# A Fourier filter followed by a maxout layer: new PSUM tiles and order for the opening, and another way out for the last output tile

## The chip, the cores and the metric

The kernel runs on one core of one Trainium2 chip. The metric is device time in microseconds of one execution; lower is better. The time before is the median of four runs.

## The reference

For each of 8 sequences (3072 positions, 256 channels) the reference filters along the sequence in the frequency domain, and the result then goes through a layer of two projections whose elementwise maximum is projected back.

```python
X = np.fft.rfft(x, axis=1)                      # x: 8 x 3072 x 256
F = (filt_r + 1j * filt_i)[None, :, :]          # 1537 x 256
y = np.fft.irfft(X * F, n=x.shape[1], axis=1)
y = y.reshape(8 * 3072, 256)
h1 = y @ w1                                     # 256 x 1024
h2 = y @ w2
out = np.maximum(h1, h2) @ w_out                # 1024 x 256
```

## The kernel before

**The mathematics.** A sequence of length 3072 is taken as 128 x 24. The transform is a product with a 128 x 128 table of sines, a second stage with 48-row tables (`U`), the filter as a product on the vector engine, and two stages back (tables `VP`, `VQ`, then `G1`, the transpose of `C1`). The maximum is computed as relu(y (w1 - w2)) w_out + y (w2 w_out). So the kernel needs `Wd` = w1 - w2 and `M` = w2 w_out, which it makes itself at the start, as it makes all tables.

**The engines.** TensorE (PE) does all products and transposes into PSUM. ScalarE (ACT) and VectorE (DVE) copy results out of PSUM. GpSimd (POOL) makes index patterns, does a few products and conversions at the start, and issues the loads of `x` and the weights and all writes of the output. SyncE (SP) issues the writes and reads of the intermediate arrays `ad`, `bt`, `zd`, `zr`. Each engine works through its own queue in the order in which the code calls it (the schedule is written by hand), and waits there for what the other engines have not finished.

**The opening (sequence 0).** While tables and data arrive, the first sequence is transformed without a trip through DRAM:

- `table_c` makes `C1` on ACT by four sine instructions, and DVE then copies it in another order to `Ct`. `tables_u` makes the angles of the second table on DVE, `sines_u` its sines on ACT.
- `expand_f(g, ri, E)` spreads 2 x 2 rows of the filter over the partitions: 16 matmuls into a PSUM tile `pf`, which engine E copies to `F`. `ri` is 0 for the real and 1 for the imaginary part.
- `first_s1(c)` is the first stage for tile c of `x` (8 matmuls into `pa`), copied to `At` by ACT. `first_t1(g, E)` transposes one group of it (8 transposes into `pt`), copied to `bt` by E.
- `tables_pe` and `tables_q` make `VP` and `VQ` (PSUM tiles `pv` and `pw`).
- `first_s2(g, pool)` is the second stage of one of 8 groups (8 matmuls into `px`). `px` holds two products, k = 0 and 1, each 2 KB per partition. They are multiplied with `F` by DVE; for three of the groups the k = 1 product is copied out by ACT to `xs` and multiplied by POOL.
- `first_s3(g, pq)` is the way back into `pz`, copied to `Zt` by ACT, behind a filler matmul (`spin`). `first_t2(j, E)` transposes `Zt` to `zr`.
- `prep_w(k, E)` transposes w2 (k = 0, 1) and multiplies it with w_out (k = 2, 3) to give `M`. `table_g` makes `G1`. On POOL, `fix_f` repairs some rows of `F`, and `prep_wd` makes w2 in bf16 and `Wd`.

**PSUM in the opening.** [...] `bank2` hands out tiles of 4 KB in two tags, `pa` and `pb`, two buffers each. Before the loop over groups the two tags take turns, so that four tiles rotate; in the loop `px` uses `pb` and everything else uses `pa`. A tile can be written again when the last reader of its predecessor has finished.

```python
ring = ["pa", "pb"]
def bank2(shape, dtype, name, tag=None):
    if tag is None:
        ring.append(ring.pop(0))
        tag = ring[-1]
    return p2.tile(shape, dtype, tag=tag, name=name)
```

**The steady part.** It has 48 output tiles of 512 rows (`tt`), 8 steps each (`j`). In each step `moe_h` computes one eighth of the hidden layer (`ph`, then `gt`) and `moe_o` a part of the previous tile's output (`po`, then `ot`). Between them, at steps that are written into `todo`, lie the transforms of later sequences: `f1` (first stage, twelve pieces, each two of which are written to `ad` by SP), `f1_read` (four reads into `bt`), `gen_f2` (second stage, filter and way back), `z_read`, and `s4`, the last stage of the transform for one tile. `f1(1, c)` is the first stage of sequence 1: four of its pieces stand before step 0, eight in steps 0 to 4, its `f1_read` at step 5, and its second stage from step 18.

**The end.** `moe_o` copies half a tile to `ot` at j = 3 and the other half at j = 7. After the second, POOL writes the 512 KB tile to the output. Behind the last tile the program ends with drains and barriers of all engines (line 733).

Of the kernel before, what the change touches and what calls it, by code (L numbers as in the profile page):

```python
# [8 lines left out]
FP32 = mybir.dt.float32  # L9
BF16 = mybir.dt.bfloat16  # L10
# [3 lines left out]
B = 8  # L14
N = 3072
D = 256
# [13 lines left out]
def kernel(  # L30
# [52 lines left out]
    init = setup.enter_context(tc.tile_pool(name="init", bufs=1))  # L83
    p2 = setup.enter_context(tc.tile_pool(name="p2", bufs=2, space=bass.MemoryType.PSUM))
    ctx.enter_context(tc.manual_schedule())
    ring = ["pa", "pb"]

    def bank2(shape, dtype, name, tag=None):
        if tag is None:
# [3 lines that stand above are left out]
# [20 lines left out]
    def expand_f(g, ri, E):  # L113
        pf = bank2([128, 2, 2, D], FP32, "pf")
        for b in range(2):
            for i in range(2):
                u = 2 * g + i
                for c in range(2):
                    for dr in range(2):
                        m, o = 4 * b + c, u  # L120
                        if dr:
                            m, o = (7 - m, 16 - u) if u else (7 - m + c, 0)
                        p0 = 64 * c + 32 * dr
                        TE.matmul(pf[p0:p0 + 32, b, i], Sel[:, m], Fs[ri][:, o], start=True, stop=True)  # L124
        evac(E, F[:, ri, :, 2 * g:2 * g + 2].rearrange("p b u d -> p b (u d)"), pf.rearrange("p b u d -> p b (u d)"))
# [62 lines left out]
    def table_c():  # L188
        V.memset(kc[:, :, 1, 0:1], 32.0)
        V.memset(kc[:, 1, 0, 0:1], 64.0)  # L190
        p128 = init.tile([128, 1], FP32)
        V.tensor_scalar(p128, pid, 1.0 / 128.0, None, OP.mult)
        uc = init.tile([128, 2, 2, T], FP32)
        rc = init.tile([128, 2, 2, T], FP32)
        V.tensor_scalar(uc[:, 0], kc[:, 0], p128, 0.25, OP.mult, OP.add)
        V.tensor_scalar(uc[:, 1], kc[:, 1], p128, 0.5, OP.mult, OP.add)
        V.tensor_scalar(uc[:, 1, 0, 0:1], kc[:, 1, 0, 0:1], p128, 0.25, OP.mult, OP.add)
        V.tensor_scalar(rc, uc, RND, RND, OP.add, OP.subtract)
        V.tensor_tensor(uc, uc, rc, OP.subtract)
        Cv = C1.rearrange("p (h c u b a) -> p a b c h u", h=4, c=2, b=2, a=2)  # L200
        for a in range(2):
            for b in range(2):
                S.activation(Cv[:, a, b], uc[:, a, b].rearrange("p (c h u) -> p c h u", c=2, h=4),
                             AF.Sin, bias=zero, scale=TWO_PI)

        V.tensor_copy(Ct.rearrange("p (b a t) -> p t b a", b=2, a=2), C1.rearrange("p (t b a) -> p t b a", b=2, a=2))

    def tables_u():

# [82 lines left out]
    def table_g():  # L292
        pg = bank2([128, 128], BF16, "pg")
        TE.transpose(pg, C1, I128)
        S.activation(G1, pg, AF.Copy)
# [132 lines left out]
    def zeros(out_, n):  # L428
        S.activation(out_, zero.rearrange("p (a b) -> p a b", a=1).to_broadcast([128] + n), AF.Copy)

    def first_s1(c):
        pa = bank2([128, 2, 2, 2, 4, T], FP32, "pa")
        for dh in range(2):
            for n in range(4):
                TE.matmul(pa[:, dh, :, :, n], xb[0, c][:, n, 128 * dh:128 * dh + 128],  # L435
                          Ct.rearrange("p (b a t) -> p b a t", b=2, a=2), start=True, stop=True)
        S.activation(At[:, :, 0:48].rearrange("p h (a n) t -> p h a (n t)", a=2)[:, :, :, 128 * c:128 * c + 128],
                     pa.rearrange("p h b a n t -> p (h b) a (n t)"), AF.Copy)

    def first_t1(g, E):  # L440
        pt = bank2([128, 2, 2, D], BF16, "pt")
        t0 = 8 * (g // 2) + 2 * (g % 2)
        for c in range(2):
            for i in range(2):
                for dh in range(2):
                    TE.transpose(pt[:, c, i, 128 * dh:128 * dh + 128],
                                 At[:, 2 * dh:2 * dh + 2].rearrange("p b m t -> p t (b m)")[:, t0 + 4 * c + i], I128)
        o = bt[0][0:ROWS, 8 * (g // 2):8 * (g // 2) + 8].rearrange("p (c u) d -> p c u d", c=2)[:, :, 2 * (g % 2):2 * (g % 2) + 2]
        evac(E, o.rearrange("p c u d -> p c (u d)"), pt[0:ROWS].rearrange("p c u d -> p c (u d)"))

    def evac(E, out_, in_):
        if E is V:
            V.tensor_copy(out_, in_)  # L453
        else:
            S.activation(out_, in_, AF.Copy)  # L455

    def first_s2(g, pool):
        px = bank2([128, 2, 2, D], FP32, "px", "pb")
        for i in range(2):
            for k, c in QUADS:  # L460
                t_ = 8 * (g // 2) + 4 * c + 2 * (g % 2) + i
                TE.matmul(px[64 * c:64 * c + 64, k, i], U[64 * k:64 * k + 48, t_],
                          bt[0][64 * k:64 * k + 48, t_], start=True, stop=True)
        if pool:
            xs = apool.tile([128, 2, D], FP32, tag="at", name="xs")
            S.activation(xs[0:FROWS], px[0:FROWS, 1], AF.Copy)  # L466
        pq = []
        for k in range(2):
            pq.append(pqpool.tile([128, 2, 2, D], BF16, tag="pq", name="pq"))
            E, src = (G, xs) if k and pool else (V, px[:, k])  # L470
            E.tensor_tensor(pq[k][0:FROWS],  # L471
                            src[0:FROWS].rearrange("p (o i) d -> p o i d", o=1).to_broadcast([FROWS, 2, 2, D]),
                            F[0:FROWS, :, k, 2 * g:2 * g + 2], OP.mult)
        return g, pq
# [58 lines left out]
    def moe_o(tt, j):  # L533
        n, half = divmod(j, 2)
        y_, g_ = yt[tt], gt[tt]
        if j == 0:
            ot[tt] = opool.tile([128, 4, D], FP32, tag="ot", name="ot")
        if j % 4 == 0:
            po[tt] = pso.tile([128, 2, D], FP32, tag="po", name="po")
        p_ = po[tt][:, n % 2]  # L540
        if half == 0:
            for dc in range(2):
                TE.matmul(p_, y_[:, dc, n], M[:, dc], start=(dc == 0), stop=False)  # L543
            js = range(0, 3)
        else:
            js = range(3, 8)
        for jj in js:
            TE.matmul(p_, g_[:, jj, 128 * n:128 * n + 128], Wo[:, jj], start=False, stop=(jj == 7))  # L548
        if j % 4 == 3:
            V.tensor_copy(ot[tt][:, n - 1:n + 1], po[tt])  # L550
        if j == 7:
            b, i = divmod(tt, 6)
            dst = out[b * N:(b + 1) * N].rearrange("(p n) d -> p n d", n=N2)
            G.dma_start(out=dst[:, 4 * i:4 * i + 4], in_=ot[tt])  # L554


    def drain(g):
# [18 lines left out]
    order = (1, 2, 3, 0, 4, 5, 6, 7)  # L576
    expand_f(1, 0, S)
    expand_f(2, 0, S)
    first_s1(0)
    expand_f(3, 0, V)  # L580
    first_s1(1)
    sines_u(0)
    expand_f(0, 0, V)
    first_s1(2)
    sines_u(1)
    expand_f(4, 0, V)
    first_s1(3)
    sines_u(2)
    expand_f(5, 0, V)
    first_s1(4)  # L590
    tables_pe()
    first_s1(5)
    tables_q(0, S)
    first_t1(1, V)
    first_t1(2, V)
    tables_q(1, S)
    first_t1(3, V)
    expand_f(1, 1, S)
    first_t1(0, V)
    expand_f(2, 1, S)  # L600
    pend = []
    ring = ["pa"]
    for n, g in enumerate(order):
        if n < 4:
            first_t1(order[n + 4], V)
        pend.append(first_s2(g, n in (0, 2, 4)))
        if n in (1, 3):
            expand_f(6 + n // 2, 0, S)
        if n < 6:
            expand_f(order[n + 2], 1, S)  # L610
        if n == 0:
            load_wo()
        if n == 1:
            fix_f()
        if n in (1, 3, 5):
            prep_wd(n // 2, *wf)
        if n > 1:
            first_s3(*pend.pop(0))
        if n in (4, 5):
            prep_w(n - 4, S)  # L620
        if n == 4:
            table_g()
        if n == 6:
            prep_w(2, S)
            prep_w(3, S)
    first_s3(*pend.pop(0))
    first_s3(*pend.pop(0))
    zr[0] = zrpool.tile([128, N2, D], BF16, tag="zr", name="zr")
    f1(1, 0, V)
    f1(1, 1, V)  # L630
    first_t2(0, V)
    setup.close()
    ps = ctx.enter_context(tc.tile_pool(name="ps", bufs=6, space=bass.MemoryType.PSUM))
    pso = ctx.enter_context(tc.tile_pool(name="pso", bufs=2, space=bass.MemoryType.PSUM))
    ypool = ctx.enter_context(tc.tile_pool(name="ypool", bufs=3))
    gpool = ctx.enter_context(tc.tile_pool(name="gpool", bufs=2))
    opool = ctx.enter_context(tc.tile_pool(name="opool", bufs=2))
    f1(1, 2, S)
    s4(0)
    f1(1, 3, V)  # L640

    todo = {}

    def plan(step, fn, *a):
        todo.setdefault(step, []).append((fn, a))
# [25 lines left out]

    for j in range(1, 6):
        plan(j - 1, first_t2, j, V)
    for c in range(4, 12):
        plan(int(0.6 * (c - 3)), f1, 1, c, (S, V)[c % 2])
    plan(5, f1_read, 1)
    plan_f2(1, spaced(18, 1.8, 9), 28, 34)
    plan_x(2, spaced(8, 4, 6))
    plan_f1(2, spaced(34, 1, 12), 46)
# [58 lines left out]
```

## Time and profile before

| | |
|---|---|
| Median of four runs | 542.48 us (541.70 to 543.44) |
| Profiled execution, its own time | 543.44 us |
| Its span in the profile | 541.5 us |
| PE busy | 512.2 us (95%) |
| ACT busy | 337.6 us (62%) |
| DVE busy | 322.3 us (60%) |
| POOL busy | 72.5 us (13%) |
| First ph matmul (step 0) | 54.44 us |
| Last output DMA issued by POOL | 531.85 us |

The span is the time from the first to the last record of the core; 1.95 us of the execution's own time lie outside it. A busy share is an average over stages: the opening, up to about 54 us, and the end behind the last matmul have to be read by themselves. Matmul ends are modelled in the profile.

### The profile page before, as it was taken

To read this page: it belongs to the slowest core of one execution; us is meant where nothing else is said; L and a number is where in the kernel's file an instruction comes from. 1 tells how busy PE (TensorE), PEld (TensorE's weight loads), DVE (VectorE), ACT (ScalarE), POOL (GpSimd) and SP (SyncE) were. 2 spreads that over 40 slices of the span, in tenths; PEclk is the share of its full clock that TensorE was granted. 3 is DMA by queue.
4 is the path that set the end of the run, shared out by engine and by line. 5 is a ranking of instruction groups with operands and counts; after the bars stand their busy time and mean duration, and the time that the engine had idled before them with its cause. 6 is when DMAs were issued, how large, how long until landed. Compare 5 with 4: busy or idle time off the path is not lost.

```text
span 541.5 us, 12518 instructions
## 1 busy us (share of the span) xinstructions
PE 512.2 (95%) x5359; PEld 349.6 (65%) x5359; DVE 322.3 (60%) x427; ACT 337.6 (62%) x591; POOL 72.5 (13%) x126
## 2 busy tenths in 40 slices
PE   6887999999999999999999899999999999999992
PEld 3655666666667666676667566666667666677771
DVE  8676669435863576448764677338764687344331
ACT  6786747865786578745775467745775565555540
POOL 6193011011101200021001200021000000000000
PEclk9799999999999999999999999999999999999997
DMA  8973496879478956599468947599466935611111
GB/s 158 286 123 61 130 164 144 206 243 207 115 231 220 216 144 186 154 220 205 122 212 207 209 117 203 149 212 209 121 204 180 170 91 134 166 40 79 79 40 77
DMA packets 67596, 87.07 MB, mean 161 GB/s; under 512 B 3986, under 2 KB 48276, under 8 KB 66452
## 3 DMA queue, kind: packets, MB, share of 16 engines
q1 hardware_dynamic: 51908, 44.31, 36.5%
q0 software_dynamic: 15632, 41.95, 29.3%
q8 instruction: 42, 0.69, 0.5%
q14 instruction: 14, 0.11, 0.1%
HBM read 53.74 MB, written 47.19 MB: 186 GB/s over the span
## 4 chain that ended last, share of the span: by engine, by line
issue 66%; POOL 6%; PE 4%; POOLq 0%
POOL out_dram L554 4%; POOL xb L101 2%; PE po L548 1%; PE ph L523 1%; PE po L543 0%; PE px L411 0%; PE py L507 0%; POOLq L733 0%; POOLq L554 0%; PE pz L392 0%; POOLq L101 0%
## 5 line engine op out<-in xcount | busy, mean ns | idle before, releaser
L528 ACT ACTIVATE gt<-ph 128x512 bf16<-128x512 f32 x307 | 181.8, 599 | 110.9 <-PE ph L523 110.0
L548 PE MATMUL po<-Wo,gt 128*128 128x256 bf16 x1536 | 229.8, 273 | 0.0
L548 PEld LDWEIGHTS <-gt 128*128 128x128 bf16 x1536 | 150.3, 98 | 57.5
L416 DVE TENSOR_TENSOR pq<-px,F 120x1024 bf16<-120x1024 f32 x112 | 131.6, 1217 | 25.6 <-PE px L411 24.7
L550 DVE COPY ot<-po 128x512 f32<-128x512 f32 x96 | 66.2, 690 | 109.4 <-PE po L548 108.8
L396 ACT ACTIVATE zt<-pz 112x512 bf16<-112x512 f32 x112 | 60.7, 594 | 45.8 <-PE pz L392 40.7
L523 PEld LDWEIGHTS <-Wd 128*128 128x128 bf16 x768 | 69.9, 98 | 25.3 <-issue 11.1
L554 POOL DMA_DIRECT2D out_dram<-ot x48 | 25.8, 537 | 442.9 <-DVE ot L550 415.6
L526 DVE TENSOR_SCALAR gt<-ph 128x512 bf16<-128x512 f32 x77 | 52.8, 686 | 35.6 <-PE ph L523 31.6
L455 ACT ACTIVATE at<-pa 128x512 bf16<-128x512 f32 x77 | 46.2, 600 | 10.5 <-PE pa L357 9.0
L357 PE MATMUL pa<-xb,C 128*128 128x512 bf16 x84 | 31.5, 381 | 1.4 <-DVE zr L453 0.8
L507 PE MATMUL py<-G,zr 128*128 128x128 bf16 x384 | 29.7, 219 | 0.7 <-DVE pq L416 0.7
L392 PE MATMUL pz<-pq,VP 56*64 56x256 bf16 x448 | 28.8, 272 | 1.6 <-DVE pq L416 1.6
L507 PEld LDWEIGHTS <-zr 128*128 128x128 bf16 x384 | 24.9, 98 | 6.0 <-issue 3.5
L392 PE MATMUL pz<-pq,VQ 56*64 56x256 bf16 x448 | 28.1, 268 | 0.0
L101 POOL DMA_DIRECT2D xb<-in_x_dram x48 | 26.0, 551 | 7.8 <-PE pa L435 4.0
L411 PE MATMUL px<-bt,U 48*64 48x256 bf16 x448 | 23.8, 281 | 2.2 <-DMA bt<-ad 2.2
L471 DVE TENSOR_TENSOR pq<-px,F 120x1024 bf16<-120x1024 f32 x13 | 15.4, 1218 | 4.1 <-ACT xs L466 1.6
L411 PEld LDWEIGHTS <-U 48*64 48x64 bf16 x448 | 8.4, 104 | 14.4 <-issue 11.8
L392 PEld LDWEIGHTS <-VP 56*64 56x64 bf16 x448 | 13.4, 106 | 3.7 <-DVE pq L416 2.2
L124 PE MATMUL pf<-Fs,Sel 96*32 96x256 bf16 x256 | 10.5, 292 | 5.2 <-DMA Fs<-in_filt_r_dram 2.8
L455 ACT ACTIVATE F<-pf 128x1024 bf16<-128x1024 f32 x12 | 12.0, 1023 | 4.9 <-PE pf L124 4.9
(359 smaller groups left out, 576.8 us busy)
## 6 DMA issues: line engine op xcount, KB each, us to landing
out_dram<-ot POOLq DMA_DIRECT2D x48, 512.0 KB, 4.2
xb<-in_x_dram POOLq DMA_DIRECT2D x48, 256.0 KB, 7.9
ad<-at SPq DMA_DIRECT2D x42, 256.0 KB
bt<-ad SPq DMA_DIRECT2D x28, 384.0 KB
zd<-zt SPq DMA_DIRECT2D x56, 192.0 KB
zr<-zd SPq DMA_DIRECT2D x14, 768.0 KB
wf<-in_moe_w_dram POOLq DMA_DIRECT2D x2, 1024.0 KB, 15.3
Fs<-in_filt_r_dram POOLq DMA_DIRECT2D x1, 768.0 KB, 6.9
```

The costliest lines, as they stand in the source:

```text
L101: G.dma_start(out=t_, in_=src[:, 4 * c:4 * c + 4, :])
L392: TE.matmul(pz[c][64 * k:64 * k + 64, i], W[64 * c:64 * c + 56, 2 * g + i, k], pq[k][64 * c:64 * c + 56, ri, i], start=(ri == 0), stop=(ri ...
L396: S.activation(zt[0:ROWS, c, o:o + 2], pz[c][0:ROWS], AF.Copy)
L416: V.tensor_tensor(pq[k][0:FROWS], px[k][0:FROWS].rearrange("p (o i) d -> p o i d", o=1).to_broadcast([FROWS, 2, 2, D]), F[0:FROWS, :, k, 2 ...
L455: S.activation(out_, in_, AF.Copy)
L507: TE.matmul(py[:, n], zr[b][:, 4 * i + n, 128 * dc:128 * dc + 128], G1, start=True, stop=True)
L523: TE.matmul(ph, Wd[:, dc, 128 * j:128 * j + 128], y_[:, dc].rearrange("p a b -> p (a b)"), start=(dc == 0), stop=(dc == 1))
L526: V.tensor_scalar(gt[tt][:, j], ph, 0.0, None, OP.max)
L528: S.activation(gt[tt][:, j], ph, AF.Relu)
L548: TE.matmul(p_, g_[:, jj, 128 * n:128 * n + 128], Wo[:, jj], start=False, stop=(jj == 7))
L550: V.tensor_copy(ot[tt][:, n - 1:n + 1], po[tt])
L554: G.dma_start(out=dst[:, 4 * i:4 * i + 4], in_=ot[tt])
```

## The change

The change has four parts.

1. **PSUM in the opening.** The ring before the loop has the one tag `pa`, so two tiles of 4 KB rotate there. The other four banks are a tag `px` with four buffers of 2 KB each: `first_s2` takes two of them, one per k, and `first_t1` takes one.
2. **Sines.** `Ct` is made by four sine instructions of its own on ACT, ahead of the four of `C1`. The copy on DVE is gone.
3. **Order.** `first_s1(4)` and `first_s1(5)` come earlier, the former copied out by DVE; `first_t1(1)` and `(2)` go around `tables_pe`; `first_t1` in the loop comes behind `first_s2` and starts one group later. `prep_w` and `table_g` leave the loop and stand among the last `first_s3`, two parts of `prep_w` with DVE. Two of the four `f1(1, c)` before step 0 move into the steps, and `f1_read(1)` goes from step 5 to step 6.
4. **The last output tile.** It is written in two halves by SP, at j = 3 and j = 7. All other tiles are written by POOL as before.

```diff
-    ring = ["pa", "pb"]
+    ring = ["pa"]
...
+        for a in range(2):
+            for b in range(2):
+                S.activation(Ct.rearrange("p (b a h c u) -> p a b c h u", b=2, a=2, h=4, c=2)[:, a, b],
+                             uc[:, a, b].rearrange("p (c h u) -> p c h u", c=2, h=4), AF.Sin, bias=zero, scale=TWO_PI)
...
-        V.tensor_copy(Ct.rearrange("p (b a t) -> p t b a", b=2, a=2), C1.rearrange("p (t b a) -> p t b a", b=2, a=2))
...
-    def first_s1(c):
+    def first_s1(c, E):
...
-        S.activation(At[:, :, 0:48].rearrange("p h (a n) t -> p h a (n t)", a=2)[:, :, :, 128 * c:128 * c + 128],
-                     pa.rearrange("p h b a n t -> p (h b) a (n t)"), AF.Copy)
+        evac(E, At[:, :, 0:48].rearrange("p h (a n) t -> p h a (n t)", a=2)[:, :, :, 128 * c:128 * c + 128],
+             pa.rearrange("p h b a n t -> p (h b) a (n t)"))
     def first_t1(g, E):
-        pt = bank2([128, 2, 2, D], BF16, "pt")
+        pt = p2.tile([128, 2, 2, D], BF16, tag="px", name="pt", bufs=4)
...
     def first_s2(g, pool):
-        px = bank2([128, 2, 2, D], FP32, "px", "pb")
+        px = [p2.tile([128, 2, D], FP32, tag="px", name="px", bufs=4) for _ in range(2)]
...
-        if j == 7:
+        if j == 7 or tt == 6 * B - 1 and j == 3:
             b, i = divmod(tt, 6)
             dst = out[b * N:(b + 1) * N].rearrange("(p n) d -> p n d", n=N2)
-            G.dma_start(out=dst[:, 4 * i:4 * i + 4], in_=ot[tt])
+            if tt < 6 * B - 1:
+                G.dma_start(out=dst[:, 4 * i:4 * i + 4], in_=ot[tt])
+            else:
+                n = n - 1
+                nc.sync.dma_start(out=dst[:, 4 * i + n:4 * i + n + 2], in_=ot[tt][:, n:n + 2])
...
-    first_s1(3)
+    first_s1(3, S)
+    first_s1(4, V)
+    first_s1(5, S)
     sines_u(2)
     expand_f(5, 0, V)
-    first_s1(4)
+    first_t1(1, V)
     tables_pe()
-    first_s1(5)
+    first_t1(2, V)
     tables_q(0, S)
-    first_t1(1, V)
-    first_t1(2, V)
+    expand_f(1, 1, S)
+    first_t1(3, V)
     tables_q(1, S)
-    first_t1(3, V)
-    expand_f(1, 1, S)
-    first_t1(0, V)
     expand_f(2, 1, S)
...
     for n, g in enumerate(order):
-        if n < 4:
-            first_t1(order[n + 4], V)
         pend.append(first_s2(g, n in (0, 2, 4)))
+        if n < 5:
+            first_t1(order[n + 3], V)
...
-        if n in (4, 5):
-            prep_w(n - 4, S)
-        if n == 4:
-            table_g()
-        if n == 6:
-            prep_w(2, S)
-            prep_w(3, S)
+    table_g()
+    prep_w(0, S)
     first_s3(*pend.pop(0))
+    prep_w(1, V)
     first_s3(*pend.pop(0))
     zr[0] = zrpool.tile([128, N2, D], BF16, tag="zr", name="zr")
-    f1(1, 0, V)
-    f1(1, 1, V)
+    prep_w(2, V)
     first_t2(0, V)
+    prep_w(3, S)
...
-    f1(1, 2, S)
     s4(0)
-    f1(1, 3, V)
+    f1(1, 0, V)
+    f1(1, 1, S)
...
-    for c in range(4, 12):
-        plan(int(0.6 * (c - 3)), f1, 1, c, (S, V)[c % 2])
-    plan(5, f1_read, 1)
+    for c in range(2, 12):
+        plan(int(0.6 * (c - 1)), f1, 1, c, (S, V)[c % 2])
+    plan(6, f1_read, 1)
```

More of the change, by code (lines that the diff above doesn't have):

```diff
@@ L461, in first_s2 @@
                 t_ = 8 * (g // 2) + 4 * c + 2 * (g % 2) + i
-                TE.matmul(px[64 * c:64 * c + 64, k, i], U[64 * k:64 * k + 48, t_],
+                TE.matmul(px[k][64 * c:64 * c + 64, i], U[64 * k:64 * k + 48, t_],
                           bt[0][64 * k:64 * k + 48, t_], start=True, stop=True)
@@ L465, in first_s2 @@
             xs = apool.tile([128, 2, D], FP32, tag="at", name="xs")
-            S.activation(xs[0:FROWS], px[0:FROWS, 1], AF.Copy)
+            S.activation(xs[0:FROWS], px[1][0:FROWS], AF.Copy)
         pq = []
@@ L469, in first_s2 @@
             pq.append(pqpool.tile([128, 2, 2, D], BF16, tag="pq", name="pq"))
-            E, src = (G, xs) if k and pool else (V, px[:, k])
+            E, src = (G, xs) if k and pool else (V, px[k])
             E.tensor_tensor(pq[k][0:FROWS],
@@ L578 @@
     expand_f(2, 0, S)
-    first_s1(0)
+    first_s1(0, S)
     expand_f(3, 0, V)
-    first_s1(1)
+    first_s1(1, S)
     sines_u(0)
     expand_f(0, 0, V)
-    first_s1(2)
+    first_s1(2, S)
     sines_u(1)
     expand_f(4, 0, V)
-    first_s1(3)
+    first_s1(3, S)
+    first_s1(4, V)
+    first_s1(5, S)
     sines_u(2)
     expand_f(5, 0, V)
-    first_s1(4)
+    first_t1(1, V)
     tables_pe()
-    first_s1(5)
+    first_t1(2, V)
     tables_q(0, S)
-    first_t1(1, V)
-    first_t1(2, V)
+    expand_f(1, 1, S)
+    first_t1(3, V)
     tables_q(1, S)
-    first_t1(3, V)
-    expand_f(1, 1, S)
-    first_t1(0, V)
     expand_f(2, 1, S)
```

## Prediction

> **What bounds the kernel now.** I read the page first: how busy each engine is, and the clock row.
>
> ```profile
> span 541.5 us, 12518 instructions
> PE 512.2 (95%) x5359; PEld 349.6 (65%) x5359; DVE 322.3 (60%) x427; ACT 337.6 (62%) x591; POOL 72.5 (13%) x126
> PE   6887999999999999999999899999999999999992
> PEclk9799999999999999999999999999999999999997
> ```
>
> PE is at nine tenths or more in slices 5 to 39 but one. The change adds and removes no matmul, so what it can move lies in the first 60 us and behind the last matmul. Next, PE's waits up to 60 us (total, times, longest):
>
> ```profile
> PE pf L124 <- DMA Fs<-in_filt_r_dram: 2.8, 1, 2.8
> PE pf L124 <- DVE F L453: 1.6, 1, 1.6
> PE pa L435 <- DMA xb<-in_x_dram: 1.4, 3, 0.7
> PE pa L357 <- DVE zr L453: 0.8, 1, 0.8
> ```
>
> and two windows of engine time (PE, PEld, DVE, ACT, POOL, clock, DMA):
>
> ```profile
> 14.56:17.97 3.41, 2.37 (x36) 1.58 (x39) 3.34 (x3) 2.19 (x4) 1.19 (x3) 0.50 1.15 229
> 17.97:21.38 3.41, 3.41 (x92) 2.71 (x85) 2.02 (x2) 2.31 (x4) 0.40 (x1) 0.50 0.96 296
> ```
>
> PE lacks data, then PSUM slots, then clock (0.50, the column behind POOL's): from 15.6 to 21.5 us it is the bound of the opening, since a group of 8 or 16 takes 1.03 us there in the timeline and 0.62 outside. Last, the end. POOL's timeline:
>
> ```profile
> 527.49 0.53 POOL L554 DMA_DIRECT2D out_dram<-ot  x1 [7.29 <-DVE ot L550]
> 531.85 0.53 POOL L554 DMA_DIRECT2D out_dram<-ot  x1 [3.83 <-DVE ot L550]
> ```
>
> The instructions of line 733, where the program ends (ns min/median/max, first and last start):
>
> ```profile
> L733 POOLq DRAIN  x3: 46/93/8877, 531.8 to 541.2; - x3
> L733 SPq DRAIN  x3: 7/7/13, 535.2 to 541.0; - x3
> ```
>
> and the window behind the last landing:
>
> ```profile
> 534.75:541.48 6.73, 0.00 (x0) 0.00 (x0) 0.00 (x0) 0.00 (x0) 0.00 (x0) 0.50 0.00 0
> ```
>
> The last write has landed at 534.75 (2.9 us after its issue) and SP has seen it at 535.2, but nothing works for 6.7 us more: POOL's drain, reached at 531.83, lasts 8.88 us, to 540.71. Barriers of 0.8 us follow. **The end is set by POOL's drain**, not by the last bytes.
>
> **The last tile.** Removed: POOL's 48th output issue. POOL's last DMA is then the one of 527.49, and its drain is reached 531.85 - 527.49 = 4.36 us earlier. Added: two 256 KB writes on SP, which has only its final waits left. The first goes out after the copy of about 529.4, under PE's last groups. The second waits for the copy that ends at 531.56. The nearest row is a 256 KB SP write in batch 1: issue 62.17, seen by SP at 64.19, 2.0 us. So 531.6 + 2.0 = 533.6, and up to 0.4 us for SP's remaining waits (0.06 each): 534.0. The drain ends later: 540.71 - 4.36 = 536.35, plus 0.8 makes a span of 537.1. **-4.4 us.** The drain's cause is not in the trace, so I bound it. If it counts from the landing of POOL's last write (534.40 in the packets; the one before ended at 531.07, a straggler), the gain is 3.3. If it shrinks, SP sets the end at 534.0 + 0.8: at most 6.7. If only the data path counts, about 1. I take 4.4, as the drain begins when POOL reaches it.
>
> Here a rule weighs against me. The Trainium skill, DMA: Bandwidth & Descriptors, Specifications, puts the first byte at about 1 us by GpSimd's path and 0.6 by SP's, and its fit (Anatomy of one DMA) is 2.0 us + bytes/436 GB/s: 3.2 us for 512 KB, 2.6 for 256 KB. By it I would estimate -1.0 in all (0.6 for size, 0.4 for path). The trace agrees on the write (2.9) but shows 6 us behind it that the rule has no term for.
>
> **The opening.** I stepped the queues forward in program order, each operation at the duration of its row, starting when its engine, inputs and PSUM slot are free, 0.04 us after what releases it. On the kernel before this gives 27.0 for the first px (trace 27.13), 53.8 for the first ph (54.44), 62.2 for the ninth, step 8 (62.79): a little short, the same stages. PE's starts, with the same clock for both:
>
> | PE group | trace, before | walk, before | walk, changed |
> |---|---|---|---|
> | pf of group 3 | 10.71 | 10.71 | 11.25 |
> | pf of group 0 | 12.55 | 12.56 | 14.21 |
> | pf of group 4 | 15.60 | 15.51 | 16.13 |
> | first_s1 of tile 5 | 20.46 | 20.37 | 19.44 |
> | pw, first half | 21.60 | 21.48 | 24.63 |
> | first_t1 of group 1 | 22.62 | 22.50 | 21.77 |
> | px, first | 27.13 | 27.04 | 27.80 |
> | px, last | 46.71 | 46.34 | 44.57 |
> | first_t2 of tile 0 | 51.28 | 50.86 | 50.86 |
> | ph, step 0 | 54.44 | 53.77 | 53.72 |
> | ph, step 8 | 62.79 | 62.16 | 62.56 |
>
> Step by step:
> - Sines. DVE loses the Ct copy (0.56) and the wait of 1.07 in front of it: its table chain starts about 1.3 us earlier and is free for F near 12.95, not 14.33. ACT gains four sines at 0.22 spacing, 0.95 us, hidden in its 2.69 us wait for the first pf; without that they would push F back by as much.
> - Ring of one tag, two slots instead of four. pf of group 3 is still evicted by DVE, now at 12.95 + 1.22 = 14.17, and the second next tile (pf of group 0) waits for it: PE stands 1.5 us. Before, the fourth next did, to 15.6. PE restarts 1.4 earlier with two groups fewer done, at 0.97 each in half clock. Then three waits of 0.4 for DVE evictions (1.22 each, one now an At that was 1.02 on ACT). first_t1 of group 1 starts 0.7 earlier.
> - Here VP is queued on DVE behind bt (0.69), and pw0 waits for it 1.06 us; ACT's VQ and F stand behind pw0. First px +0.8.
> - xs of the first px now stands behind F(2, 1) on ACT (1.02), so POOL starts at 29.6, not 28.3. POOL then has 16.4 us without a gap (three products of 2.13, Wo 0.95, fix_f 2.4, w2b 2.0, two Wd of 2.34). Product 3 ends at 44.0, and first_s3 of group 4 waits for it, 1.4 us.
> - prep_w and table_g leave the loop: 1.1 us of transposes, 1.9 of pm, two 1.02 evictions on ACT (one becomes 0.69 on DVE). The last px comes 1.8 earlier; behind the loop they cost it back: first_t2 at 50.9 in both. Their users come later (M first at 63.2).
> - first_t1 uses the four px banks, moved one step later; its one wait for px is 0.5. The banks per k save nothing direct: k already had its own 2 KB.
> - Two f1 go from before step 0 into steps 0 to 6: 2 x 0.22 = 0.4 on a full PE, where before they filled waits. Their SP writes and the four reads of f1_read (step 6) shift by some 1.2 us. The first half of bt (0.79 MB; queue 1 moved 1.34 MB from 64 to 74 us) lands near 71.5, used at 74.5: covered by 3 us, beyond which each microsecond is lost on PE.
>
> **Opening +0.4 us.** The clock is the open term. The skill, TensorE: Matmul & The Clock Gate, Part 1, throttles after an idle window of some 3.4 us; by that rule this opening (longest pause 2.8) is never halved, and the walk at full clock gives 60.4 and 61.3: +0.9. Its section on a second failure mode, PSUM-queue depth-cycling, speaks against this change: short pauses between groups make the clock oscillate. The trace has it halved, and 69% busy did not lift it while 100% did. The walk has 89%, 77%, then about 100% in the same three windows: half clock to 17.97, 21.38 or 24.80 gives -0.4, +0.4, +0.7. I keep +0.4, range -0.4 to +1.6.
>
> **Sum.** The profiled execution took 543.44, 1.95 beyond its span. 543.44 - 4.4 + 0.4 = 539.4. It is the slowest of four, 0.96 above the median of 542.48, so against the median 538.5.
>
> **Rivals.** A measurement of this kernel can tell about 0.3% (1.6 us) from no change.
> - A, drain from POOL's last issue: 538.5, own range 537.3 to 540. Chance 0.60.
> - B, drain from landing: 542.48 - 3.3 + 0.4 = 539.6, 0.15. The one drain in the trace fits it as well as A: it ends 6.3 us behind the last packet.
> - C, drain shrinks and SP sets the end: 542.48 - 6.7 + 0.4 = 536.2, 0.08. For it: POOL's other two drains, with no DMA just before, take 46 and 93 ns. Against it: even if landing were all it waited for, 6 us of it lie behind the landing.
> - D, drain stays tied to the program's last bytes: -1.0 + 0.4 gives 541.9, no change, 0.09. Against it: POOL no longer owns those bytes.
> - E, slower: the two-slot ring keeps PE at half clock. Place: from 14.56 on, no window busy enough. Walked with half clock to 45 us, step 8 comes at 68.6, +6.5: 542.48 - 4.4 + 6.5 = 544.6. It decides if the clock stays halved past about 43 us; to 28 it costs 1.6. Against it: from 21.4 to 24.8 PE is full in the walk. 0.08.
>
> Faster: A, B, C less a little, 0.81; same 0.11; slower 0.08. The range, 536.6 to 541.3, holds A, B and most of D's near side and leaves out E and part of C.
>
> **What would show it.** POOL's last output DMA near 527.5 and line 733's long drain starting there, about 8.9 us, its end the span's end less 0.8; two SP writes on line 560. A drain ending over 9.5 us after POOL's last issue, or SP's last wait ending the span, breaks step one. In the opening: the pf wait on DVE F near 1.5 us ending at 14.2; Ct gone from DVE; pw0 waiting for VP; POOL's first product near 29.6; the first ph within 1 us of 54.4. A clock of 0.50 past 25 us, or a px L411 wait on bt at 74, would make me wrong.

## The result and the profile after

| | before | changed |
|---|---|---|
| Median, all runs | 542.49 us (53 runs, 540.83 to 545.41) | 540.49 us (32 runs, 538.52 to 544.00) |
| Profiled execution, its own time | 543.44 us | 541.3 us |
| Its span | 541.5 us | 539.4 us |

The ratio is 0.9961, 95% interval 0.9949 to 0.9973: the change gains 2.1 us (1.5 to 2.8). The prediction was 538.5, a gain of 4; the time lies in its range of 536.6 to 541.3, at about half of the gain. Ratios and their intervals leave out executions more than 1.5% above the fastest of their kernel (one in "The old ring with the new order", three in "Four slots up to the loop"); medians are over all executions.

The page's lines on the span, PE and the granted clock:

```profile
span 539.4 us, 12524 instructions
PE 514.5 (95%) x5359; PEld 351.1 (65%) x5359; DVE 322.9 (60%) x427; ACT 336.5 (62%) x594; POOL 72.1 (13%) x125
PE   6788999999999999999999999999999999999995
PEclk9799999999999999999999999998999999999998
```

PE is full over the same stretch as before; the clock row has a dip in slice 28 that it did not have. The half clock in slice 2 is in both.

The end first. POOL's timeline and the drains of line 734, where the changed program ends (ns min/median/max, first and last start):

```profile
529.68 0.53 POOL L557 DMA_DIRECT2D out_dram<-ot  x1 [7.29 <-DVE ot L552]
```

```profile
L734 POOLq DRAIN  x3: 46/102/8792, 529.7 to 539.0; - x3
L734 SPq DRAIN  x3: 7/7/7, 536.1 to 538.7; - x3
```

POOL's last output issue is now that of tile 47 of 48, at 529.68. The drain is reached there and lasts 8.79 us, to 538.45; SP is through at 536.2 and waits. PE's last group of ph matmuls, before and changed:

```profile
525.32 0.59 PE L523 MATMUL ph<-y__8003,Wd 128*128 128x512 bf16 x2
```

```profile
527.51 0.59 PE L525 MATMUL ph<-y__8014,Wd 128*128 128x512 bf16 x2
```

The second matmul of each starts 0.22 us later. Behind its start the program now takes 539.44 - 527.73 = 11.7 us; before it took 541.49 - 525.54 = 15.95. That is 4.2 us less.

But PE comes to the end 2.2 us later than before. Its starts in the profiled executions say where:

| ph of step | before | changed | difference |
|---|---|---|---|
| 0 | 54.44 | 54.22 | -0.22 |
| 8 | 62.79 | 63.03 | +0.23 |
| 180 | 283.83 | 284.06 | +0.23 |
| 230 | 348.18 | 347.67 | -0.50 |
| 256 | 379.30 | 381.55 | +2.25 |

In this execution the opening costs only 0.2. The other 2 us are one event near 366 us, in PE's timeline and a window of engine time (the column behind POOL's is the granted clock):

```profile
365.21 0.41 PE L413 MATMUL px<-bt,U 48*64 48x256 bf16 x7 [1.82 <-DMA bt<-ad]
```

```profile
365.90:369.30 3.40, 3.40 (x17) 1.86 (x15) 3.31 (x4) 0.80 (x2) 0.00 (x0) 0.50 1.08 258
```

PE waits 1.82 us for the read of `bt`, and then runs 3.4 us at half clock. In the kernel before, the same wait is 0.75 and no half clock follows. The change does not touch these steps, and in the profiles of all experiments below the stretch from step 230 to step 256 takes 31.0 to 31.9 us; here it takes 33.9. No other profile has it, so it is taken as an accident of this one execution. This profile therefore does not show where 2 us of the median went; the experiments do.

For the opening, PE's waits of the first 62 us:

```profile
PE pf L124 <- DMA Fs<-in_filt_r_dram: 2.9, 1, 2.9
PE pf L124 <- ACT At L457: 1.1, 1, 1.1
PE pw L302 <- DVE VP L292: 0.8, 1, 0.8
...
PE pz L487 <- POOL pq L473: 0.5, 1, 0.5
```

The waits that were walked are there: pf of group 0 for its slot, pw for VP behind bt, pz for POOL's product. The first is not quite as walked: PE stands 1.1 us, to 14.37, where 1.5 us to 14.2 was expected, and the last to release it is ACT's copy of At; DVE's F, which was to release it, had ended at 14.18. The waits for x data (1.4 in total before) are gone: PE comes later than the data now.

### The profile page after: what moved, and what is told of

Read it like the earlier page. It is cut to its first block, busy times and chain, and to the rows that moved or that the text cites. A ratio compares the mean times of both kernels' runs of the same rounds, so it can differ in the third digit from the quotient of the medians.

```text
span 539.4 us, 12524 instructions
## 1 busy us (share of the span) xinstructions
PE 514.5 (95%) x5359; PEld 351.1 (65%) x5359; DVE 322.9 (60%) x427; ACT 336.5 (62%) x594; POOL 72.1 (13%) x125
## 4 chain that ended last, share of the span: by engine, by line
PE 70%; DMA 5%; DVE 1%; ACT 0%; SPq 0%; issue 0%
PE po L550 26%; PE ph L525 26%; PE po L545 6%; DMA bt<-ad 4%; PE pz L394 4%; PE px L413 3%; PE py L509 3%; PE pa L359 3%; DMA ad<-at 2%; DVE pq L418 1%; ACT at L457 0%; DVE ot L552 0%; SPq L369 0%
## 5 line engine op out<-in xcount | busy, mean ns | idle before, releaser
L525 PEld LDWEIGHTS <-Wd 128*128 128x128 bf16 x768 | 70.1, 98 | 25.1 <-issue 10.7
L413 PE MATMUL px<-bt,U 48*64 48x256 bf16 x448 | 23.8, 281 | 2.5 <-DMA bt<-ad 2.5
```

What stands on the lines that cost most here:

```text
L413: TE.matmul(px[k][64 * c:64 * c + 64, i], U[64 * k:64 * k + 48, t_], bt_[64 * k:64 * k + 48, t_], start=True, stop=True)
L525: TE.matmul(ph, Wd[:, dc, 128 * j:128 * j + 128], y_[:, dc].rearrange("p a b -> p (a b)"), start=(dc == 0), stop=(dc == 1))
```

## The experiments

Two theories stood at the start. T: the tail gives its 4.3 us every time, and the new opening takes about 2 of them back in the typical execution. U: the opening costs nothing, the tail gives only 2. When T held, the question was what in the opening costs it: the time at half clock or the order, the PSUM tiles or both. Each execution's time at half clock is 2 x (1 - its mean granted clock) x its span. It includes what the clock is halved behind the last matmul (8.1 us in the profiled execution before, 2.9 in the changed one).

### The tail alone

```diff
 (kernel before)
-        if j == 7:
+        if j == 7 or tt == 6 * B - 1 and j == 3:
...
-            G.dma_start(out=dst[:, 4 * i:4 * i + 4], in_=ot[tt])
+            if tt < 6 * B - 1:
+                G.dma_start(out=dst[:, 4 * i:4 * i + 4], in_=ot[tt])
+            else:
+                n = n - 1
+                nc.sync.dma_start(out=dst[:, 4 * i + n:4 * i + n + 2], in_=ot[tt][:, n:n + 2])
```

> The kernel before with part 4 alone: the last tile leaves by SP in two halves. Theory T (the tail gives its full 4.3 us in every execution, and the new opening takes about 2 of them back in the typical one): -4.3 us against before, ratio 0.992. Rival U (the opening costs nothing, the tail gives only about 2 us in the typical execution): -2.0 us, ratio 0.9963. Both: POOL's drain begins at its 47th output issue and lasts 8.8 us.

537.40 us (6 runs) beside 542.83 for before; ratio 0.9891 (0.9856 to 0.9927), a gain of 5.9 us (4.0 to 7.8). T's 4.3 lies inside, U's 2.0 outside. In its trace the stretch behind the last ph group is 535.74 - 524.23 = 11.5 us, 4.4 less than before; the drain starts at the last issue:

```profile
526.18 0.53 POOL L555 DMA_DIRECT2D out_dram<-ot  x1 [7.29 <-DVE ot L550]
```

```profile
L737 POOLq DRAIN  x3: 46/102/8792, 526.2 to 535.5; - x3
```

### The tail put back

```diff
 (changed kernel)
-        if j == 7 or tt == 6 * B - 1 and j == 3:
+        if j == 7:
...
+            G.dma_start(out=dst[:, 4 * i:4 * i + 4], in_=ot[tt])
```

> The changed kernel with part 4 undone: POOL writes the last tile, the new opening stays. Theory T: +2 us against before (ratio 1.004), with more time at half clock in the opening than before. Rival U: 0.0 to +0.3 us, as the profiled executions of before and after have step 8 only 0.2 us apart (ratio 1.000).

545.26 us (22 runs) beside 542.83; ratio 1.0041 (1.0022 to 1.0061): the new opening costs 2.2 us (1.2 to 3.3). T holds. Against the changed kernel, which has the same opening, the ratios differ by 0.0080: the SP tail gives 4.3 us there. The median time at half clock is 26.1 us; before has 15.1 in the same job. The windows of its profile:

```profile
16.00:20.00 4.00, 3.29 (x37) 2.50 (x36) 2.27 (x2) 2.69 (x3) 1.06 (x2) 0.50 0.98 229
20.00:24.00 4.00, 3.54 (x53) 2.71 (x54) 2.34 (x2) 1.79 (x4) 0.53 (x1) 0.50 1.02 409
24.00:28.00 4.00, 3.94 (x92) 2.37 (x85) 2.35 (x4) 1.06 (x2) 0.00 (x0) 0.50 1.11 243
28.00:32.00 4.00, 4.00 (x58) 2.34 (x57) 1.54 (x2) 3.19 (x4) 0.00 (x0) 0.68 1.10 204
```

PE is 82 to 98% busy from 16 to 28 us and its clock stays halved all the same, to 30.5 us by the clock records. Step 8 starts at 65.54 here, at 62.79 before.

### Two tiles by SP

```diff
 (changed kernel)
-        if j == 7 or tt == 6 * B - 1 and j == 3:
+        if j == 7 or tt >= 6 * B - 2 and j == 3:
...
-            if tt < 6 * B - 1:
+            if tt < 6 * B - 2:
```

> The changed kernel with the last two tiles written by SP, each in halves. POOL's last output issue then lies 8.3 us before PE's last group's copy instead of 4.1. If the drain lasts 8.8 us from POOL's last DMA, it ends before SP has seen the last half, and SP's waits set the end: 2.3 us less than the changed kernel (538.2 us against 540.5). If the drain is tied to the program's last bytes or lasts 8.8 us whenever it starts late, no change.

537.29 us (6 runs) beside 542.83; ratio 0.9892 (0.9857 to 0.9926), where the changed kernel has 0.9961. The drains:

```profile
L734 POOLq DRAIN  x3: 46/93/8711, 519.5 to 534.2; - x3
L734 SPq DRAIN  x3: 7/7/7, 533.7 to 534.0; - x3
```

The long drain runs from 519.53 to 528.24. The end is now SP's: its last wait is over at 533.7, and the span ends at 534.7. POOL's last issue, at 519.55, lies 11.9 us ahead of the end of DVE's last copy (8.3 was expected). Behind the last ph group there are 9.3 us, 2.4 less than in the changed kernel, as expected; the ratios differ by more (3.7 us), with intervals wide enough for 2.4. The drain is not tied to the program's last bytes (the prediction's rival D).

### A late POOL copy

```diff
 (kernel with two tiles by SP)
                 nc.sync.dma_start(out=dst[:, 4 * i + n:4 * i + n + 2], in_=ot[tt][:, n:n + 2])
+                if tt == 6 * B - 1 and j == 7:
+                    G.tensor_copy(ot[tt - 1][:, 0, 0:64], ot[tt][:, 3, 0:64])
```

> As the kernel with the last two tiles on SP, and in addition one small POOL copy (128 x 64) behind the last DVE copy, so that POOL's drain is reached about 12 us after its last DMA. The copy overwrites rows of a tile that has already been written out. If the drain waits for something that POOL's last DMA leaves behind for 8.8 us, it is short here (under 1 us) and the span is about that of the kernel with two tiles on SP. If a drain costs 8.8 us by itself whenever POOL has issued DMAs, it lasts 8.8 us from about 534 and the span is about 4 to 5 us longer.

One execution, 543.88 us. POOL's end and its drain:

```profile
520.75 0.53 POOL L557 DMA_DIRECT2D out_dram<-ot  x1 [7.74 <-DVE ot L552]
532.71 0.24 POOL L562 COPY ot<-ot 128x64 f32<-128x64 f32 x1 [11.42 <-DVE ot L552]
```

```profile
L736 POOLq DRAIN  x3: 46/102/8431, 532.7 to 541.6; - x3
```

POOL's last DMA lies 12 us back, and the drain takes 8.4 us all the same. Counted from the end of POOL's last instruction it is 541.12 - 532.95 = 8.2 us here and 538.45 - 530.21 = 8.2 in the changed kernel. So the drain does not wait for POOL's last DMA: **it takes 8.2 us behind POOL's last instruction, a DMA issue in one kernel and a copy in the other.** Behind the last ph group this execution takes 15.5 us, 6.2 more than with two tiles by SP (4 to 5 were expected). The prediction's rivals B and C fall with that.

### More filler matmuls

```diff
 (changed kernel)
-    spin(bank2([128, 2, 512], FP32, "pd")[:, 0], 14)
+    spin(bank2([128, 2, 512], FP32, "pd")[:, 0], 24)
```

> The changed kernel with 24 instead of 14 filler matmuls ahead of the first pf, so that PE does not stand from 5.8 to 8.6 us. Theory T1 (the new opening costs its 2 to 2.5 us by time at half clock): half clock before 40 us falls from 10 to 20 us to under 7, and the time falls by about 2 us against the changed kernel (to about 538.5 on its runs, ratio to before about 0.9925). Rival T2 (two slots and later evictions cost it whatever the clock): unchanged within 0.5 us, ratio about 0.996.

539.06 us (6 runs) beside 542.68; ratio 0.9934 (0.9912 to 0.9957): 1.5 us less than the changed kernel by the ratios. The median time at half clock falls from 20.5 to 15.6 us. That is nearer to T1 than to T2, but its interval overlaps the changed kernel's, and in the profile step 8 starts at 63.04, no earlier than in the changed kernel's. There the half clock is 6.8 us long, from 13.6 to 20.4; in the typical execution it is longer than the 7 us that T1 expected. Filling the pause ahead of the first pf removes part of the half clock and not all of it.

### The old ring with the new order

```diff
 (changed kernel)
-    ring = ["pa"]
+    ring = ["pa", "pb"]
...
-        pt = p2.tile([128, 2, 2, D], BF16, tag="px", name="pt", bufs=4)
+        pt = bank2([128, 2, 2, D], BF16, "pt")
...
-        px = [p2.tile([128, 2, D], FP32, tag="px", name="px", bufs=4) for _ in range(2)]
+        px = bank2([128, 2, 2, D], FP32, "px", "pb")
```

> The changed kernel with part 1 undone: four rotating tiles before the loop, px in one 4 KB tile, first_t1 from the common ring; sines, order and the SP tail stay. If the two-slot ring is what keeps PE in short pauses and so at half clock: about -5 us against before (ratio 0.991), as with the tail alone. If the new order is the cause: still about -2 to -3 us (ratio 0.995).

Neither: 547.72 us (8 runs), ratio 1.0074 (1.0044 to 1.0103), with the SP tail in it. Up to the loop it is the fastest of all: first px at 23.97 us, 28.01 in the changed kernel. In the loop it starves:

```profile
PE pf L124 <- ACT F L457: 2.9, 3, 1.1
PE pz L314 <- ACT F L457: 2.3, 2, 1.1
...
PE pt L448 <- ACT F L457: 0.8, 1, 0.8
```

```profile
32.00:44.00 12.00, 9.74 (x163) 5.61 (x163) 5.94 (x7) 5.18 (x6) 8.58 (x7) 0.50 0.35 48
```

first_t1, pf and pz share two slots there and each waits for ACT's copy of F. PE pauses, its clock is halved from 30.4 to 57.7 us, and the first ph comes at 62.63. The new order needs the px banks in the loop.

### Sines and tail

```diff
 (kernel before, with the tail by SP)
+        for a in range(2):
+            for b in range(2):
+                S.activation(Ct.rearrange("p (b a h c u) -> p a b c h u", b=2, a=2, h=4, c=2)[:, a, b], ...
...
-        V.tensor_copy(Ct.rearrange("p (b a t) -> p t b a", b=2, a=2), C1.rearrange("p (t b a) -> p t b a", b=2, a=2))
```

> The kernel before with part 2 (four sines for Ct on ACT, no copy on DVE) and part 4 (last tile by SP). The DVE table chain starts 1.3 us earlier, so PE's wait for the third pf ends 1.3 us earlier. If that counts: 1 us less than the tail alone (about 536.4 where it was 537.4, ratio 0.987). If the time at half clock or the At evictions decide anyway: the same as the tail alone within 0.5 us (ratio 0.989).

536.64 us (6 runs), ratio 0.9889 (0.9863 to 0.9915); the tail alone had 0.9891 in another job. The ratios show no difference, the profile a clear one: step 8 starts at 61.18, 1.6 us ahead of before, with the same 6.8 us at half clock. Part of that may be place: here they lie at 8.3 to 15.1 us, a stretch in which PE is only about 60% busy in the kernel before, so that slower matmuls can fill waits. The timing can't settle a gain of 1 us.

### Old opening, two tiles, more fillers

```diff
 (kernel before)
-    spin(bank2([128, 2, 512], FP32, "pd")[:, 0], 14)
+    spin(bank2([128, 2, 512], FP32, "pd")[:, 0], 24)
 (and the last two tiles by SP)
```

> The kernel before with its own opening, the last two tiles by SP and 24 instead of 14 filler matmuls. If the gains add: tail of one tile -4.3 to -5.4, second tile -2 (the drain then ends ahead of SP's last wait), less half clock in the opening -1 to -2: 534 to 535 us, ratio 0.984 to 0.987. If the half clock of the old opening is not due to the pause of 5.8 to 8.6 us: 535.5 us, ratio about 0.988.

536.30 us (6 runs), ratio 0.9885 (0.9856 to 0.9915). In the profile the second tile takes its 2.4 us off the end (9.1 us behind the last ph group); the ratio is only 0.3 us below that of the tail alone, and the two intervals are too wide to tell. The fillers gain nothing that shows: the half clock comes later (16.6 to 23.5 us), and the first ph at 54.34 is where it was.

### The square of ring and order

```diff
 (kernel before, with the sines and the tail by SP)
-    ring = ["pa", "pb"]
+    ring = ["pa"]
...
-        pt = bank2([128, 2, 2, D], BF16, "pt")
+        pt = p2.tile([128, 2, 2, D], BF16, tag="px", name="pt", bufs=4)
...
-        px = bank2([128, 2, 2, D], FP32, "px", "pb")
+        px = [p2.tile([128, 2, D], FP32, tag="px", name="px", bufs=4) for _ in range(2)]
```

> The kernel before with parts 1, 2 and 4: the new PSUM tiles with the old order of the opening. It completes the square of ring and order. Theory W: the two slots ahead of the loop cost what they cost in the changed kernel, so about 540 to 541 us (ratio 0.996), first px at 28 us or later. Rival X (the order is the cost, the ring is not): as with the old ring, 536.6 us (0.989).

542.28 us (22 runs), ratio 0.9997 (0.9981 to 1.0013). The new ring costs the old order 5.9 us by the ratios, the whole gain of the tail and more than W expected (540 to 541). All four have the sines and the SP tail; the times at half clock are medians:

| | old order | new order |
|---|---|---|
| old ring | 0.9889, 6.4 us at half clock | 1.0074, 35.5 us |
| new ring | 0.9997, 23.8 us | 0.9961, 20.5 us |

The windows of the two kernels in the left column, old ring first:

```profile
12.00:16.00 4.00, 4.00 (x61) 2.62 (x54) 3.46 (x8) 3.02 (x4) 1.62 (x3) 0.61 1.15 214
16.00:20.00 4.00, 2.68 (x102) 2.03 (x100) 2.76 (x3) 3.57 (x7) 1.06 (x2) 1.00 1.02 229
20.00:24.00 4.00, 3.56 (x49) 2.60 (x49) 2.37 (x4) 3.25 (x4) 0.53 (x1) 1.00 1.01 401
```

```profile
12.00:16.00 4.00, 2.75 (x40) 1.71 (x32) 2.08 (x6) 2.73 (x3) 1.62 (x3) 0.50 1.17 218
16.00:20.00 4.00, 3.29 (x44) 2.41 (x44) 2.45 (x2) 2.38 (x3) 1.06 (x2) 0.50 1.00 228
20.00:24.00 4.00, 3.55 (x96) 2.81 (x89) 1.88 (x2) 2.11 (x4) 0.53 (x1) 0.50 1.01 409
```

With four slots PE is busy through 12 to 16 us and the clock comes back; with two it pauses 0.4 to 1.1 us at a time for a slot, the clock stays halved to 25.7, and the first px comes at 30.0 us (25.5 with the old ring). Either ring is slow with the other's order: the new one with the old order by 5.9 us, the old one with the new order by 6.1.

### Four slots up to the loop, px banks in it

```diff
 (changed kernel)
-    p2 = setup.enter_context(tc.tile_pool(name="p2", bufs=2, space=bass.MemoryType.PSUM))
+    early = ExitStack()
+    p2 = early.enter_context(tc.tile_pool(name="p2", bufs=2, space=bass.MemoryType.PSUM))
...
-    ring = ["pa"]
+    ring = ["pa", "pb"]
...
-        pt = p2.tile([128, 2, 2, D], BF16, tag="px", name="pt", bufs=4)
+        pt = bank2([128, 2, 2, D], BF16, "pt") if len(ring) > 1 else p2.tile([128, 2, 2, D], BF16, tag="px", name="pt", bufs=4)
...
     pend = []
+    early.close()
+    p2 = setup.enter_context(tc.tile_pool(name="p3", bufs=2, space=bass.MemoryType.PSUM))
```

> The changed kernel with its PSUM pool opened twice: four rotating 4 KB tiles up to the loop, as before the change, and the new two 4 KB tiles with four px banks from the loop on. Order, sines and SP tail stay. Theory W (the two slots ahead of the loop make PE pause, so that the half clock lasts past 20 us; the new order is good in the loop only with the px banks): first px at 24 us instead of 28, first ph near 50 to 51, and about 3 to 4 us less than the changed kernel (536.5 to 537.5, ratio 0.989). Rival X (the order itself is the cost): no more than 1 us less than the changed kernel (ratio 0.995).

537.62 us (22 runs), ratio 0.9911 (0.9893 to 0.9928): 2.7 us less than the changed kernel by the ratios, and 10.7 us at half clock in the median. The mean of all 22, its three longest included (544.24 to 545.03, with 34.8 to 38.0 us at half clock), is 0.9933 of the mean before, only 1.5 us less than the changed kernel. W's time is nearly met; X's limit of 1 us is passed either way. The old opening with the sines (0.9889) is no slower, so the new order gains nothing that shows even with its slots back. The first px comes at 25.6 and not at 24: the new pool has to wait for the last users of the old one.

```profile
PE px L465 <- ACT F L458: 1.7, 1, 1.7
```

The first ph of its profiled execution is at 56.5, far from the 50 to 51 expected: in that execution the clock is halved again from 26.6 to 43.6 us, behind this pause. And it stays so although PE is full by the profile:

```profile
26.58:29.99 3.41, 3.41 (x52) 2.09 (x52) 3.09 (x4) 1.20 (x2) 3.11 (x3) 0.50 1.12 209
29.99:33.41 3.42, 3.42 (x52) 1.93 (x44) 2.90 (x4) 2.43 (x3) 2.00 (x3) 0.50 1.20 199
33.41:36.82 3.41, 3.41 (x65) 2.12 (x65) 1.40 (x3) 1.83 (x2) 3.41 (x4) 0.50 0.68 92
```

So pauses of PE are not all that keeps the clock halved. 5 of the 22 executions have more than 24 us at half clock, and they run from 536.06 to 545.03, a spread that only the old ring with the new order exceeds.

### What gained, and no other

```diff
 (kernel before: sines of part 2, and)
-        if j == 7:
+        if j == 7 or tt >= 6 * B - 2 and j == 3:
...
+            if tt < 6 * B - 2:
```

> The kernel before with its own ring and order, with the sines of part 2 and the last two tiles by SP in halves: the parts that gained, and no other. If the gains add, 2.3 us less than the kernel with sines and one tile: 534.3 us, ratio about 0.985. If the second tile gains nothing here, 536.6 (0.989).

534.52 us (4 runs) beside 542.04; ratio 0.9850 (0.9824 to 0.9876), better than both kernels and 2.1 us below the sines with one tile by the ratios, where 2.3 was expected. In its profiled execution the clock is never halved ahead of the last matmul: first ph at 51.69, step 8 at 60.05.

## Why the prediction came out as it did

**The direction and the tail were right.** Predicted was a drain from POOL's last output issue, 8.9 us long, 4.4 us earlier against PE's end. Measured: 8.8 us, and 4.2 to 4.5 us less behind the last ph group in three pairs of profiles (before and changed, before and the tail alone, the tail put back and changed). SP's 2.0 us for its last half was 2.05 (issue 533.78, seen at 535.83). The estimate that was weighed against it, from the Trainium skill, DMA: Bandwidth & Descriptors (Specifications and Anatomy of one DMA), was 1.0 in all; the tail alone gave at least 4.0. The late copy shows why: the 6 us behind the write belong to POOL's drain and not to a DMA. The time alone would not have told: 540.49 lies outside rival A's own range (537.3 to 540) and nearer to B's 539.6, while the drain is A's.

**The step that failed is the last term of the opening: "Opening +0.4 us", with the half clock ending at 21.38.** It measured +2.2 (1.2 to 3.3), above the range of -0.4 to +1.6 given for it, though the lower end of the interval reaches into it. The walk itself held, since in the profiled execution of the changed kernel the clock came back at 21.2, about where it was assumed: first px 28.01 (walked 27.80), last px 44.33 (44.57), first ph 54.22 (53.72), step 8 63.03 (62.56). DVE was free at 12.96 (12.95), POOL's first product at 29.82 (29.6), the chain of POOL without a gap, s3 of group 4 waiting for it 0.5 instead of 1.4. At full clock the walk had 60.4 for the old opening's step 8; the last experiment, with the sines in addition, has 60.05 (the walked 61.3 for the new opening at full clock was met by no run). What was wrong is the time at half clock that the typical execution has:

| new ring and order: kernel | half clock in its opening | step 8 |
|---|---|---|
| changed | 10.2 us | 63.03 |
| two tiles by SP | 13.7 us | 63.62 |
| late POOL copy | 17.1 us | 64.24 |
| tail put back | 20.5 us | 65.54 |

The four share one opening, and step 8 comes later the longer the half clock lasts. The executions say the same: over the 32 of the changed kernel, time and time at half clock go together (correlation 0.84, 0.25 us per us), and the opening with the tail put back has 11.0 us more of it than before in the median. The sign that was named for this, a clock of 0.50 past 25 us, is not in the changed kernel's profile but in that with the tail put back (30.5).

I took a window of 89% or about 100% modelled PE time as enough to lift it. In the profile with the tail put back a window from 23.7 to 27.1 us that is 98% busy lifts nothing. So rival E, whose sum keeps A's 4.4 us for the tail, was the right mechanism at about a third of its size: 542.49 - 4.4 + 2.2 gives 540.3, and 540.49 was measured.

**The rule that spoke against the change was underweighted.** The Trainium skill's section on PSUM-queue depth-cycling (TensorE: Matmul & The Clock Gate) has the clock going down when PE pauses shortly between groups as it cycles through PSUM. Here part 1 (two slots for four ahead of the loop, and the px banks) raises the median time at half clock from 6.4 to 23.8 us and the ratio from 0.9889 to 0.9997 in the old order, with nothing else changed; in the new order four slots ahead of the loop lower it from 20.5 to 10.7. That the ring costs time at half clock is shown. That it does so by PE's pauses is argued: they come together in the profiles, but three full windows in a row did not lift the half clock in one of them. The rule of the page's Part 1, an idle window of some 3.4 us, explains none of it: no pause of PE up to 54 us is longer than 2.9 us in these profiles.

**Part by part.** The sines were costed at nothing on ACT, and that holds. What the earlier DVE chain gives beside the two slots was not tried by itself; with the old ring step 8 is 1.6 us ahead in one profile, and the timing shows no gain outside its interval. "The banks per k save nothing direct" missed that the new order can't do without them in the loop: with the old tiles it costs 6.1 us more than with the new ones by the ratios. Moving two f1 cost the 0.4 us that was walked: from step 0 to step 8 it is 8.8 us in the changed kernel and 8.35 in the kernel before. The read of bt for step 18 was covered: PE has no wait for it at 74 us.

What stays open: the tail alone gained 4.0 to 7.8 us, where the profiles show 4.4. The lower end fits, and so do the 4.3 us between the changed kernel and the one with the tail put back; whether the rest is chance was not tried. Nor was it found what lifts the half clock: it ended behind windows of 84% (changed kernel) and 89% (more filler matmuls), and not behind one of 98% (tail put back) and three of 100% (four slots up to the loop).

## What to carry to other kernels

Read who ends the program before tuning its last bytes: here it was POOL's drain of 8.2 us. Giving the last two tiles to SP, so that the drain runs under PE's last matmuls, took 1.5% together with the sines; the new opening took half of the tail's gain back. Before PSUM is cut into other tiles, count the slots that rotate in every stage, not only in the one that gains: fewer slots cost this kernel 5.9 us, and 17 us more at half clock came with them. Where the clock changes at another place in every execution, one profile is one draw; judge by the median of many executions, and use the mean granted clock of each as the second number.

## What was not expected of the hardware

- The drain of POOL at the program's end takes 8.2 to 8.3 us behind POOL's last instruction, also when that is a copy of 0.24 us and its last DMA lies 12 us back. The drains of SP, ACT, PE and DVE take 0.01 to 2.2 us.
- The start of the first full-clock period lies anywhere from 4.1 to 6.7 us after the first record in these profiles, and all later changes of the clock follow at multiples of 3.41 us. So the clock is first halved at 8.0 to 10.9 us in the four profiles that share the new opening, each time at another place in the same work. The kernel before has between 5 and 22 us at half clock and runs from 540 to 548 us.
- In the changed kernel a wait of 1.8 us of PE in the middle of the run was followed by 3.4 us at half clock. It is one event; with four slots up to the loop the clock stayed halved through three windows of 3.41 us in which PE was full.
